# Routed attention and a bilinear feed-forward layer: one product moved to second place at the change of batch element, a combination made later, an assignment spread over two groups, and sums in another order

## The chip, the cores and the metric

The kernel runs on one core of a Trainium2 chip. The metric is the device time of one execution in microseconds (us). The core has TensorE (matrix products, PE in the profile; PEld is its loading of weights), VectorE (DVE), ScalarE (ACT), GpSimd (POOL) and SyncE (SP), which starts most transfers here. SBUF holds the working data, and products land in PSUM.

## The reference

Routed attention: queries and keys get the nearest of 16 centroids of their head, and a query sees only keys of its own centroid. Then a bilinear feed-forward layer.

```python
batch, n_heads, seq, head_dim = (4, 8, 768, 64)   # 16 centroids per head
q_assign = argmax(q_n @ c_n); k_assign = argmax(k_n @ c_n)
scores = where(q_assign == k_assign, q @ k.T / 8, -1e9)
attn = softmax(scores)
x = (attn @ v) laid out as (3072 tokens, 512)
a = x @ w_a            # 512 x 1536
b = x @ w_b
return (a * b) @ w_out # 1536 x 512
```

All of it is float32; the weights come as float64 bits and are rounded on the chip.

## The kernel before

The attention goes over 16 pairs of heads (4 per batch element). A pair has two halves of 384 queries, and a half has six blocks of 128 keys; two blocks make a *group* g, so a pair takes six groups (l = 0 to 5) and the whole attention 96. In group g TensorE makes the scores of g, ScalarE their exponentials, VectorE (from pair 4 on partly GpSimd) adds up the probabilities of g-1, and TensorE weighs the values with them. The feed-forward layer of the batch element before is cut into pieces, which fill TensorE between the groups. The main loop, cut:

```python
for g in range(NG + 3):
    p, l = divmod(g, GPP)                       # GPP = 6 groups per pair
    if l == 0:
        ready = prep_steps(p + 1)               # the next pair's preparation
    ...
    if 0 < g < NG:
        score(now)
    check_inverses()
    if 0 < g <= NG:
        for u in before:
            add_up(u)                           # acc, L570
    flush_w()                                   # end of a weight's rounding
    if 0 < g <= NG:
        weigh(before)
    if g < NG:
        ready[l]()
    late = int(g > EARLY)
    if g % 3 == late and 0 < g - late:
        denominators(*divmod(g // 3 - 1, 2))    # L604
    ...                                         # rounding of weights due now
    if halved:
        todo.extend(normalize(*ph))
    if ffn:
        credit += PER_GROUP[...]
        while len(ffn) > least and credit > 0:
            cost, piece = ffn.popleft()
            credit -= cost
            piece()
            if todo:
                todo.popleft()()
            round_next()
    ...
    while todo:
        todo.popleft()()
    if halved:
        ffn_ready(*ph)                          # a finished element's pieces
```

**Up projection of batch elements 1 to 3.** Blocks of the weights (A) and of x (X) are multiplied by a scheme with seven products instead of eight, for twelve parts (six column blocks of each weight). It needs sums and differences of blocks: S1 to S4 of the weights (a part each) and T1 to T4 of x (once for the batch element). VectorE makes both.

```python
def combine_x(b):                               # the first piece of an element
    up_room()
    x = xTs[b]
    for c in range(2):
        x11, x12 = x[:, c, 0:HB], x[:, c, HB:S]
        x21, x22 = x[:, c + 2, 0:HB], x[:, c + 2, HB:S]
        t2, t3, t4 = (W[t][c] for t in ("T2", "T3", "T4"))
        for out, l, r in ((t3, x22, x12), (x12, x12, x11), (t2, x22, x12),
                          (t4, t2, x21)):
            nc.vector.tensor_tensor(out=out, in0=l, in1=r, op=ALU.subtract)   # L725
```

In the profile T2 and T3 lie in tiles named raw, T4 in size, T1 in xT itself. S1 to S4 are made at L747 (raw, comb, size). The pieces of a part run in the order p1, p6, p2, p7, p4, p5, p3, each with one product (L764) into one of three PSUM buffers (m), which is free again once its result has been added:

```python
def p1():  ps = product("11", "11"); box["11"] = ...; nc.scalar.copy(out=box["11"], in_=ps)
def p6():  ps = product("S2", "T2"); ...; add(box["12"], box["11"], ps)
def p2():  add(box["11"], box["11"], product("12", "21")); done("11", 0, i)
def p7():  ps = product("S3", "T3"); ...; add(box["22"], box["12"], ps)
def p4():  ps = product("22", "T4"); ...; add(box["21"], box["22"], ps, ALU.subtract)
...
for n, (half_1, half_2, ps) in enumerate(parts):
    ps[0] = both(*([half_1] if n == 0 else []), half_2, ps[0])   # S1 to S4 before p1
    if n + 1 < len(parts):
        ps[4] = both(ps[4], parts[n + 1][0])
    pieces += [(2 * HB, f) for f in ps]
```

When a batch element changes, combine_x is put ahead of the last two pieces of the down projection of the element before (L883, additions at L889), and p1 and p6 of the new element follow these:

```python
ffn.insert(len(ffn) - FREE_ROOM, (0, lambda: combine_x(b)))      # FREE_ROOM = 2
ffn.extend(ffn_ups(b, h) + ffn_downs(b, lambda: h))
```

Behind the loop the same pieces run on without attention; between p7 and p4 of the last element's first part one small product (L1109) counts rows that are far off and takes a PSUM buffer of the same three.

**The sums.** For the pairs of the first batch element (p < HP = 4) the last block's probabilities aren't added to acc but summed by TensorE itself, as a second term:

```python
def denominators(p, hf):
    ps = ps_m.tile([P, 512], FP32, name="m")
    acc = accs.pop((p, hf))
    terms = [acc]
    if p < HP:
        terms.append(probs[p * UPP + hf * NJ + NJ - 1])
    for n, t in enumerate(terms):
        for a in range(2):
            nc.tensor.matmul(out=ps[a * D:(a + 1) * D, 0:HB], lhsT=ones,
                             rhs=t[:, a, :], start=(n == 0),
                             stop=(n == len(terms) - 1))              # L604
    den = acc[:, 0, :]
    ...
```

**The assignment.** Pairs from 4 on are prepared by blocks, in six steps, one for each group of the pair before; pair 4's fall into g=18 to 23. Step l=2 has four VectorE instructions (L487, L488, L489, L492), l=3 the one-hot code (half on GpSimd at L470, half on VectorE at L472), l=4 its transpose (L476) and eight transfers to ohT, which the scores of the pair read.

Of the kernel before, what the change touches and what calls it, by code (L numbers as in the profile page):

```python
# [14 lines left out]
ALU = mybir.AluOpType  # L15
AX = mybir.AxisListType
# [120 lines left out]
def short_path(nc, tc, ctx, c, cn, centroids_in, casts, n_far, q, k, v,  # L137
# [3 lines left out]
    B, H, S, D = q.shape  # L141
    NC = 16
    DM, DF = moe_w_a.shape
    NJ = S // P
    HP = H // 2
# [3 lines left out]
    HB = S // 2  # L149
# [93 lines left out]
    first = load_first()  # L243
# [199 lines left out]
    def prep_by_blocks(p):  # L443

        qkTs[p] = qtp.tile([P, 2 * S], FP32, name="qkT")
        ohTs[p] = ohT_bufs[p % 2]
        NG = 24
        QT = slice(0, P // 2)
        KT = slice(P // 2, P)
        shape = (P, NG, NC)  # L450
        sim = simp.tile([P, NG, NC], FP32, name="sim")
        mx = small.tile([P, NG], FP32, name="mx")
        first = small.tile([P, NG], FP32, name="first")
        oh = oh_all[:, 0:3].rearrange("p n (g c) -> p (n g) c", c=NC)
        ohT = oh_all[:, 3:6].rearrange("p n e -> p (n e)")
        top = lambda t: t[:, :, None].broadcast_to(shape)
        v = nc.vector

        def across(w):
            v.transpose(out=qkTs[p][:, w * S:(w + 1) * S],  # L460
                        in_=qks[p][:, w].rearrange("p j d -> p (j d)"))

        def sims_across():
            v.transpose(out=sim.rearrange("p g c -> p (g c)"),
                        in_=sims[p][:, 0:HB])

        def one_hot():


            nc.gpsimd.tensor_tensor(out=oh[KT], in0=sim[KT], in1=top(first)[KT],  # L470
                                    op=ALU.subtract)
            v.tensor_tensor(out=oh[QT], in0=sim[QT], in1=top(first)[QT],  # L472
                            op=ALU.is_equal)

        def one_hot_across():
            v.transpose(out=ohT, in_=oh.rearrange("p g c -> p (g c)"))  # L476
            for a in range(2):
                for kq in range(4):
                    r = 32 * kq + a * NC
                    nc.sync.dma_start(  # L480
                        out=ohTs[p][a * D:a * D + NC, kq * HB:(kq + 1) * HB],
                        in_=ohT[r:r + NC, :])

        return [
            [lambda: across(0), lambda: across(1)],
            [sims_across],
            [lambda: v.tensor_reduce(out=mx, in_=sim, axis=AX.X, op=ALU.max),  # L487
             lambda: v.tensor_tensor(out=sim, in0=sim, in1=top(mx), op=ALU.is_ge),  # L488
             lambda: v.tensor_tensor(  # L489
                 out=sim, in0=sim, in1=rank_far[:, None, :].broadcast_to(shape),  # L490
                 op=ALU.mult),
             lambda: v.tensor_reduce(out=first, in_=sim, axis=AX.X, op=ALU.max)],  # L492
            [one_hot],
            [one_hot_across],
            [],
        ]

    def prep_steps(p):
        if p >= NPAIR:
# [24 lines left out]
    UPP = 2 * NJ  # L524
# [69 lines left out]
    def denominators(p, hf):  # L594


        ps = ps_m.tile([P, 512], FP32, name="m")
        acc = accs.pop((p, hf))
        terms = [acc]
        if p < HP:  # L600
            terms.append(probs[p * UPP + hf * NJ + NJ - 1])
        for n, t in enumerate(terms):
            for a in range(2):
                nc.tensor.matmul(out=ps[a * D:(a + 1) * D, 0:HB], lhsT=ones,  # L604
# [3 lines that stand above are left out]
        n = 4 * p + 2 * hf  # L608
        nc.scalar.activation(out=den, in_=ps[:, 0:HB], func=AF.Copy,
                             accum_out=stat[:, n:n + 1])  # L610
        den_of[p, hf] = acc
# [104 lines left out]
    def combine_x(b):  # L716
        up_room()
        x = xTs[b]
        for c in range(2):
            x11, x12 = x[:, c, 0:HB], x[:, c, HB:S]  # L720
            x21, x22 = x[:, c + 2, 0:HB], x[:, c + 2, HB:S]
            t2, t3, t4 = (W[t][c] for t in ("T2", "T3", "T4"))
            for out, l, r in ((t3, x22, x12), (x12, x12, x11), (t2, x22, x12),
                              (t4, t2, x21)):
                nc.vector.tensor_tensor(out=out, in0=l, in1=r, op=ALU.subtract)  # L725

    def ffn_ups(b, h):
# [3 lines left out]
             "T1": [x[:, c, HB:S] for c in (0, 1)],  # L731
             "21": [x[:, c, 0:HB] for c in (2, 3)],
             "22": [x[:, c, HB:S] for c in (2, 3)]}

        def products(w_sb, i, is_a):
            N2 = NF // 2
            A = {m + n: [w_sb[:, c, f * P:(f + 1) * P] for c in cs]
                 for m, f in (("1", i), ("2", i + N2))
                 for n, cs in (("1", (0, 1)), ("2", (2, 3)))}
            box = {}  # L740

            def combine(name, l, r, op):

                at = {"S1": 1, "S2": 2, "S3": 0, "S4": 3}[name]
                dst = W["slots"][at]
                for c in range(2):
                    nc.vector.tensor_tensor(out=dst[c], in0=l[c], in1=r[c], op=op)  # L747
                A[name] = dst

            def half_1():  # L750
                combine("S1", A["21"], A["22"], ALU.add)
                combine("S2", A["S1"], A["11"], ALU.subtract)

            def half_2():
                combine("S3", A["11"], A["21"], ALU.subtract)
                combine("S4", A["12"], A["S2"], ALU.subtract)
                s = W["slots"]
                W["slots"] = [s[1], s[2], s[0], s[3]]

            def product(l, r):  # L760
                ps = ps_m.tile([P, 512], FP32, name="m")
                rhs = X[r] if r in X else W[r]
                for c in range(2):
                    nc.tensor.matmul(out=ps[:, 0:HB], lhsT=A[l][c], rhs=rhs[c],  # L764
                                     start=(c == 0), stop=(c == 1))
                return ps[:, 0:HB]

            def place(k, f):
                if is_a:
                    return h[k][:, f, :]  # L770
                return hap.tile([P, HB], FP32, name="ha")

            def add(out, in0, ps, op=ALU.add):
                nc.vector.tensor_tensor(out=out, in0=in0, in1=ps, op=op)  # L774

            def done(name, k, f):
                if not is_a:
                    to = h[k][:, f, :]
                    nc.gpsimd.tensor_tensor(out=to, in0=to, in1=box[name],  # L779
                                            op=ALU.mult)  # L780

            def p1():
                if not h:
                    h.extend(hp_.tile([P, NF, HB], FP32, name="h")
                             for _ in range(2))
                ps = product("11", "11")
                box["11"] = place(0, i)
                nc.scalar.copy(out=box["11"], in_=ps)

            def p6():  # L790
                ps = product("S2", "T2")
                box["12"] = place(1, i)
                add(box["12"], box["11"], ps)

            def p2():
                add(box["11"], box["11"], product("12", "21"))
                done("11", 0, i)

            def p7():
                ps = product("S3", "T3")  # L800
                box["22"] = place(1, i + N2)
                add(box["22"], box["12"], ps)

            def p4():
                ps = product("22", "T4")
                box["21"] = place(0, i + N2)
                add(box["21"], box["22"], ps, ALU.subtract)
                done("21", 0, i + N2)

            def p5():  # L810
                ps = product("S1", "T1")
                add(box["12"], box["12"], ps)
                add(box["22"], box["22"], ps)
                done("22", 1, i + N2)

            def p3():
                add(box["12"], box["12"], product("S4", "22"))
                done("12", 1, i)

            return half_1, half_2, [p1, p6, p2, p7, p4, p5, p3]  # L820

        parts = [products(w_sb, i, w_sb is wa_sb) for i in range(NF // 2)
                 for w_sb in (wa_sb, wb_sb)]
        pieces = []
        for n, (half_1, half_2, ps) in enumerate(parts):
            ps[0] = both(*([half_1] if n == 0 else []), half_2, ps[0])
            if n + 1 < len(parts):
                ps[4] = both(ps[4], parts[n + 1][0])
            pieces += [(2 * HB, f) for f in ps]
# [126 lines left out]
    def both(*fs):  # L956
        return lambda: [f() for f in fs]
# [380 lines left out]
```

## Time and profile before

Three runs took 1072.07, 1072.6 and 1073.93 us (median 1072.6). The profiled execution has a span of 1072.3 us and a mean granted TensorE clock of 0.995.

| engine | busy us | share of the span | instructions |
|---|---|---|---|
| VectorE | 708.9 | 66% | 1402 |
| GpSimd | 354.6 | 33% | 329 |
| ScalarE | 260.0 | 24% | 501 |

TensorE's line is shown with the prediction. Transfers take 17.8% of the time of the 16 engines that move data. The first group with feed-forward pieces is g=23, near 117 us; batch elements change near 408, 666 and 904 us.

How to read the lines: `out<-in` names the tiles written and read, the shapes are partitions x elements, `xN` is the number of instructions merged into the line. A float32 product stands as two records, so a product of the up projection with its two chunks has four. The wait in brackets is the idle time ahead of the instruction and what ended it.

### The profile page before, as it was taken

What the parts mean: (1) busy time and instruction counts of PE and PEld (TensorE: products, weight loads), DVE (VectorE), ACT (ScalarE), POOL (GpSimd) and SP (SyncE); (2) the same over time, 40 slices, a digit from 0 to 9 for tenths busy, and PEclk for the clock granted to TensorE, in tenths of its full rate; (3) what the DMA queues carried; (4) which work ended last, traced back from release to release, by engine and by line L of the source; (5) the groups of instructions that cost most, each with busy time, mean ns of one, the idle gap of its engine ahead of it and who ended that gap; (6) DMA issues with size and microseconds to landing.
All of it is one profiled execution on the core that took longest, in us unless ns stands there. A gap on an engine that the chain in (4) does not pass through costs nothing.

```text
span 1072.3 us, 13072 instructions
## 1 busy us (share of the span) xinstructions
PE 1054.1 (98%) x4756; PEld 607.3 (57%) x4756; DVE 708.9 (66%) x1402; ACT 260.0 (24%) x501; POOL 354.6 (33%) x329
## 2 busy tenths in 40 slices
PE   8999999999999999999999999999999999999997
PEld 5444445554557664454545766455455687555686
DVE  5778877787857446666667746667665745676762
ACT  4665333233322221212122121221212200000000
POOL 1111345454533232434445422344344410221200
PEclk9999999999999999999999999999999999999999
DMA  5334243525130210202020030300000000000000
GB/s 169 91 63 108 83 103 101 125 67 139 61 47 20 43 37 14 45 4 45 3 46 1 24 65 14 55 1 19 1 4 1 6 30 25 0 1 1 0 31 32
DMA packets 120504, 46.18 MB, mean 43 GB/s; under 512 B 106608, under 2 KB 115824, under 8 KB 120432
## 3 DMA queue, kind: packets, MB, share of 16 engines
q1 hardware_dynamic: 120016, 44.85, 17.8%
q8 instruction: 39, 0.64, 0.2%
q10 hardware_dynamic: 416, 0.43, 0.1%
q14 instruction: 33, 0.27, 0.1%
HBM read 37.78 MB, written 6.29 MB: 41 GB/s over the span
## 4 chain that ended last, share of the span: by engine, by line
PE 93%; DVE 6%; issue 1%; DMA 0%; POOL 0%; ACT 0%; DVEq 0%; POOLq 0%
PE m L764 30%; PE m L883 19%; PE s L540 14%; PE O L581 12%; PE m L664 12%; PE m L604 3%; PE m L358 1%; DVE raw L725 1%; DVE raw L747 1%; PE m L342 1%; DVE acc L570 0%; DVE xT L725 0%; DVE size L725 0%; DVE ha L774 0%; DVE sim L407 0%
## 5 line engine op out<-in xcount | busy, mean ns | idle before, releaser
L549 ACT ACTIVATE pt<-s 128x768 f32<-128x768 f32 x192 | 145.3, 809 | 314.6 <-PE s L540 260.6
L570 POOL TENSOR_TENSOR acc<-acc,pt 128x384 f32<-128x384 f32 x144 | 152.2, 1071 | 59.7 <-ACT pt L549 43.5
L779 POOL TENSOR_TENSOR h<-h,ha 128x384 f32<-128x384 f32 x72 | 72.7, 1018 | 235.6 <-DVE ha L774 234.1
L581 PE MATMUL O<-pt,v 128*64 128x384 f32 x768 | 145.1, 499 | 0.0
L540 PE MATMUL s<-qkT 64*128 64x384 f32 x768 | 141.1, 487 | 0.0
L774 DVE TENSOR_TENSOR ha<-ha,m 128x384 f32<-128x384 f32 x126 | 66.8, 546 | 74.1 <-PE m L764 73.3
L774 DVE TENSOR_TENSOR h<-h,m 128x384 f32<-128x384 f32 x126 | 67.3, 548 | 71.8 <-PE m L764 71.0
L570 DVE TENSOR_TENSOR acc<-acc,pt 128x384 f32<-128x384 f32 x96 | 73.9, 796 | 37.2 <-POOL acc L570 35.1
L581 PEld LDWEIGHTS O<-pt,v 128*64 128x64 f32 x768 | 46.6, 136 | 86.9 <-issue 85.3
L540 PEld LDWEIGHTS s<-qkT 64*128 64x128 f32 x768 | 71.3, 189 | 32.0 <-issue 1.1
L883 PE MATMUL m<-wo_sb,h 128*128 128x256 f32 x384 | 87.5, 382 | 0.0
L636 POOL TENSOR_TENSOR xT<-xT,acc 128x384 f32<-128x384 f32 x32 | 33.0, 1033 | 153.5 <-DVE acc L631 119.5
L883 PEld LDWEIGHTS m<-wo_sb,h 128*128 128x128 f32 x384 | 72.1, 190 | 16.0 <-issue 4.2
L764 PE MATMUL m<-raw 128*128 128x384 f32 x192 | 70.2, 488 | 0.9 <-DVE ha L774 0.9
L664 PE MATMUL m<-xT,wa_sb 128*128 128x384 f32 x192 | 67.1, 492 | 0.0
L664 PE MATMUL m<-xT,wb_sb 128*128 128x384 f32 x192 | 66.8, 491 | 0.0
L883 PE MATMUL m<-xT,h 128*128 128x256 f32 x288 | 65.4, 382 | 0.1
L883 PEld LDWEIGHTS m<-xT,h 128*128 128x128 f32 x288 | 54.1, 190 | 11.7 <-issue 1.7
L764 PE MATMUL m<-xT,wa_sb 128*128 128x384 f32 x144 | 53.0, 491 | 0.0
L764 PE MATMUL m<-xT,size 128*128 128x384 f32 x144 | 52.8, 490 | 0.0
L764 PE MATMUL m<-xT,wb_sb 128*128 128x384 f32 x144 | 52.8, 490 | 0.0
L664 PEld LDWEIGHTS m<-xT,wa_sb 128*128 128x128 f32 x192 | 35.5, 190 | 29.4 <-issue 3.6
(164 smaller groups left out, 1451.6 us busy)
## 6 DMA issues: line engine op xcount, KB each, us to landing
raw<-in_moe_w_a_dram SPq DMA_DIRECT2D x12, 512.0 KB, 4.3
raw<-in_moe_w_b_dram SPq DMA_DIRECT2D x12, 512.0 KB, 3.5
raw<-in_moe_w_out_dram SPq DMA_DIRECT2D x12, 512.0 KB, 3.2
qk<-in_q_dram SPq DMA_DIRECT2D x48, 96.0 KB, 2.9
qk<-in_k_dram SPq DMA_DIRECT2D x48, 96.0 KB, 3.5
v<-in_v_dram SPq DMA_DIRECT2D x24, 192.0 KB, 3.8
out_dram<-rest SPq DMA_DIRECT2D x24, 128.0 KB, 1.7
v<-in_v_dram SPq DMA_DIRECT2D x4, 384.0 KB, 4.5
```

What stands on the lines that cost most here:

```text
L342: nc.tensor.transpose(out=ps[:, n * P:(n + 1) * P], in_=qks[p][:, w, j].rearrange("p a d -> p (a d)"), identity=ident)
L540: nc.tensor.matmul(out=s[:, a, 0:HB], lhsT=Ts[p][r, S + j * P:S + (j + 1) * P], rhs=Ts[p][r, hf * HB:(hf + 1) * HB], start=start, stop=not ...
L549: nc.scalar.activation(out=pt, in_=s[:, :, 0:HB], func=AF.Exp, scale=SCALE)
L570: eng.tensor_tensor(out=acc[:, a, :], in0=probs[u - 1][:, a, :] if j == 1 else acc[:, a, :], in1=probs[u][:, a, :], op=ALU.add)
L581: nc.tensor.matmul(out=O_of[0][a * D:(a + 1) * D, 0:HB], lhsT=vs[p][:, a, j, :], rhs=probs[u][:, a, :], start=(j == 0), stop=(j == NJ - 1))
L604: nc.tensor.matmul(out=ps[a * D:(a + 1) * D, 0:HB], lhsT=ones, rhs=t[:, a, :], start=(n == 0), stop=(n == len(terms) - 1))
L636: nc.gpsimd.tensor_tensor(out=x, in0=x, in1=den, op=ALU.mult)
L664: nc.tensor.matmul(out=ps[:, 0:HB], lhsT=w_sb[:, ch, f * P:(f + 1) * P], rhs=xTs[b][:, ch, t0:t0 + HB], start=(ch == 0), stop=(ch == NCH - 1))
L764: nc.tensor.matmul(out=ps[:, 0:HB], lhsT=A[l][c], rhs=rhs[c], start=(c == 0), stop=(c == 1))
L774: nc.vector.tensor_tensor(out=out, in0=in0, in1=ps, op=op)
L779: nc.gpsimd.tensor_tensor(out=to, in0=to, in1=box[name], op=ALU.mult)
L883: nc.tensor.matmul(out=ps[:, 0:HN], lhsT=A[l][f // 3][:, f % 3, :], rhs=B[r][f // 2][:, f % 2, :], start=(f == 0), stop=(f == N2 - 1))
```

## The change

It has four parts. (1) In the first part of each batch element's up projection, the product of p2, which reads neither an S nor a T, is made right after p1's, ahead of p6's; its addition stays in p2. (2) T4, which only p4 reads, is made with p2 rather than with the other combinations of x. Both are meant for TensorE's wait when the batch element changes. (3) Pair 4's assignment is spread over two groups, two instructions each, and its one-hot code moves to the group of the transpose. (4) In the sums the last probabilities come first and acc second, so that TensorE can begin before acc is complete.

```diff
-        return [
-            [lambda: across(0), lambda: across(1)],
-            [sims_across],
-            [lambda: v.tensor_reduce(out=mx, in_=sim, axis=AX.X, op=ALU.max),
-             ...                                     # the four, as below
-            [one_hot],
-            [one_hot_across],
-            [],
-        ]
+        assign = [
+            lambda: v.tensor_reduce(out=mx, in_=sim, axis=AX.X, op=ALU.max),
+            lambda: v.tensor_tensor(out=sim, in0=sim, in1=top(mx), op=ALU.is_ge),
+            lambda: v.tensor_tensor(
+                out=sim, in0=sim, in1=rank_far[:, None, :].broadcast_to(shape),
+                op=ALU.mult),
+            lambda: v.tensor_reduce(out=first, in_=sim, axis=AX.X, op=ALU.max)]
+        if p == HP:
+            return [[lambda: across(0), lambda: across(1)], [sims_across],
+                    assign[:2], assign[2:], [one_hot, one_hot_across], []]
+        return [[lambda: across(0), lambda: across(1)], [sims_across],
+                assign, [one_hot], [one_hot_across], []]
...
         if p < HP:
-            terms.append(probs[p * UPP + hf * NJ + NJ - 1])
+            terms.insert(0, probs[p * UPP + hf * NJ + NJ - 1])
...
-            for out, l, r in ((t3, x22, x12), (x12, x12, x11), (t2, x22, x12),
-                              (t4, t2, x21)):
+            for out, l, r in ((t3, x22, x12), (x12, x12, x11), (t2, x22, x12)):
                 nc.vector.tensor_tensor(out=out, in0=l, in1=r, op=ALU.subtract)
...
+        def combine_t4():
+            for c in range(2):
+                nc.vector.tensor_tensor(out=W["T4"][c], in0=W["T2"][c],
+                                        in1=X["21"][c], op=ALU.subtract)
...
+            def p2_ahead():
+                box["P2"] = product("12", "21")
+
             def p2():
-                add(box["11"], box["11"], product("12", "21"))
+                ps = box.pop("P2") if "P2" in box else product("12", "21")
+                add(box["11"], box["11"], ps)
                 done("11", 0, i)
...
-        for n, (half_1, half_2, ps) in enumerate(parts):
+        for n, (half_1, half_2, p2_ahead, ps) in enumerate(parts):
             ps[0] = both(*([half_1] if n == 0 else []), half_2, ps[0])
+            if n == 0:
+                ps[1] = both(p2_ahead, ps[1])
+                ps[2] = both(combine_t4, ps[2])
```

More of the change, by code (lines that the diff above doesn't have):

```diff
@@ L482, in one_hot_across @@
                         in_=ohT[r:r + NC, :])
-        return [
-            [lambda: across(0), lambda: across(1)],
-            [sims_across],
-            [lambda: v.tensor_reduce(out=mx, in_=sim, axis=AX.X, op=ALU.max),
[L488 to L492, printed above, removed]
-            [one_hot],
-            [one_hot_across],
-            [],
-        ]
+        assign = [
[10 more added lines that the diff above has]
+                assign, [one_hot], [one_hot_across], []]
     def prep_steps(p):
@@ L720, in combine_x @@
             x11, x12 = x[:, c, 0:HB], x[:, c, HB:S]
-            x21, x22 = x[:, c + 2, 0:HB], x[:, c + 2, HB:S]
-            t2, t3, t4 = (W[t][c] for t in ("T2", "T3", "T4"))
-            for out, l, r in ((t3, x22, x12), (x12, x12, x11), (t2, x22, x12),
-                              (t4, t2, x21)):
+            x22 = x[:, c + 2, HB:S]
+            t2, t3 = W["T2"][c], W["T3"][c]
+            for out, l, r in ((t3, x22, x12), (x12, x12, x11), (t2, x22, x12)):
                 nc.vector.tensor_tensor(out=out, in0=l, in1=r, op=ALU.subtract)
@@ L818, in p3 @@
                 done("12", 1, i)
-            return half_1, half_2, [p1, p6, p2, p7, p4, p5, p3]
+            return half_1, half_2, p2_ahead, [p1, p6, p2, p7, p4, p5, p3]
         parts = [products(w_sb, i, w_sb is wa_sb) for i in range(NF // 2)
```

## The prediction

> **What bounds the kernel now.** I read the page's busy times first, then TensorE's table of waits, then the timeline around each large wait, and last the granted clock of the stretches behind them. Page part 1 (busy us, share of the span, instructions) and the two largest lines of TensorE's waits (total us, times, longest):
>
> ```profile
> PE 1054.1 (98%) x4756; PEld 607.3 (57%) x4756; DVE 708.9 (66%) x1402; ACT 260.0 (24%) x501; POOL 354.6 (33%) x329
> ```
> ```profile
> PE m L764 <- DVE comb L747: 4.8, 3, 2.2
> PE m L604 <- DVE acc L570: 2.9, 5, 1.7
> ```
>
> TensorE is the bound: of a span of 1072.3 us it is idle for 18.2. No product is added or removed, so only idle time, and time in which it ran slowly, can change. The two lines are what the change aims at: product p6 at the start of a batch element's up projection (L764), and the sums behind the softmax (L604). First the transition to batch element 1 (group g=52), from the timeline (start, us, engine, ..., idle before):
>
> ```profile
> 400.25 3.85 POOL L570 TENSOR_TENSOR acc<-acc,pt 128x384 f32<-128x384 f32 x3
> ...
> 403.28 1.23 DVE L725 TENSOR_TENSOR size<-raw,xT 128x384 f32<-128x384 f32 x1
> ...
> 404.89 1.45 PE L764 MATMUL m<-xT,wa_sb 128*128 128x384 f32 x4
> ...
> 406.20 0.56 DVE L725 TENSOR_TENSOR size<-raw,xT 128x384 f32<-128x384 f32 x1
> ...
> 408.20 0.48 DVE L747 TENSOR_TENSOR comb<-raw,wa_sb 128x128 f32<-128x128 f32 x2
> ...
> 408.54 1.62 PE L764 MATMUL m<-raw,comb 128*128 128x384 f32 x4 [2.20 <-DVE comb L747]
> ...
> 410.09 0.82 PE L540 MATMUL s<-ohT 64*128 64x384 bf16 x4
> ...
> 410.70 2.75 PE L540 MATMUL s<-qkT 64*128 64x384 f32 x8
> ```
>
> TensorE ends p1 at 404.89 + 1.45 = 406.34 and waits 2.20 us for S2 (written to comb), because VectorE still works through the eight subtractions of L725; the two that make T4 (size) are no part of what p6 reads. The last two lines show a second loss: twelve score records that take 1.72 us everywhere else in the chain take 3.30 here. The granted clock (PEclk, the number after the bracket) says why:
>
> ```profile
> core 0: us, PE busy (x), PEclk, DMA share, GB/s
> 408.50:410.00 1.50, 1.46 (x4) 0.97 0.09 23
> 410.00:411.50 1.50, 1.50 (x9) 0.50 0.07 16
> 411.50:413.00 1.50, 1.50 (x8) 0.50 0.09 23
> ```
>
> Then the sums, at g=3 (the same picture stands at g=9 and g=15) and at g=21:
>
> ```profile
> 29.56 1.02 DVE L570 TENSOR_TENSOR acc<-acc,pt 128x384 f32<-128x384 f32 x2
> ...
> 30.16 1.01 PE L604 MATMUL m<-acc,ones 128*64 128x384 f32 x3 [0.32 <-DVE acc L570]
> ```
> ```profile
> 107.98 1.66 DVE L570 TENSOR_TENSOR acc<-acc,pt 128x384 f32<-128x384 f32 x2
> 108.23 0.99 POOL L470 TENSOR_TENSOR oh<-sim,first 64x384 bf16<-64x384 f32 x1 [4.36 <-DVE first L492]
> ...
> 108.58 0.86 PE L604 MATMUL m<-acc,ones 128*64 128x384 f32 x2 [1.67 <-DVE acc L570]
> ...
> 109.70 0.54 PE L604 MATMUL m<-acc,ones 128*64 128x384 f32 x1 [0.26 <-DVE acc L570]
> ```
>
> The sums start with acc, whose last addition VectorE makes after the assignment of the next pair. At g=21 that addition is slow as well: its two halves take 1.66 us, since L470 runs on GpSimd between them.
>
> [...] here a wait of 2.20 us is followed by half clock, and one of 1.67 us (g=21) by clock 1.00. So I take the border to lie between those two. [...] a subtraction takes 1.23 us while L570 runs on GpSimd, 0.56 without. [...] So an early T4 delays S2, and a late T4 delays what stands behind it.
>
> **Part A: product p2 second, T4 later, at g=52 and again 257 us on (batch element 2).** VectorE before: eight subtractions from 399.35, four at about 1.25 us beside GpSimd's additions (which end at 404.10) and four at 0.58 from start to start; then the one-hot transpose and two additions of the down projection; S2 at 408.50. Two subtractions fewer: the first step of the second chunk moves into the slow stretch, so four stay slow, and two quick ones go: 2 x 0.59 = 1.18 us; S2 comes at 407.3. TensorE: p2 needs no combination, only a PSUM buffer, which the down projection's addition frees; that addition moves from 407.17 up to 406.0 and ends near 406.4. So p2 starts at 406.42, where TensorE stood idle, takes 1.29 us (products in a row start 1.29 us apart: 416.22, 417.51, 418.80), and p6 starts at 407.7, after S2. What is left of the wait is 0.1 us, and with it the drop of the clock goes.
> Worth: before, from the end of p1 to the end of the next scores 413.46 - 406.34 = 7.12 us for p6 and scores, whose undisturbed sum is 1.29 + 1.72 = 3.01. Lost: 4.1 (2.20 wait, 0.33 on p6, 1.58 on the scores). Batch element 2, from p1's end at 662.10 + 1.45 to the scores' at 668.57 + 2.11: 7.13, lost 4.1 (2.20, 1.52, 0.39). Gain 4.0 each, **8.0 us**. T4 is made in the next group during the scores (VectorE is free from about 410.2; T4 is done by 411.4 and p2's addition by 412.0), while p4, which reads it and needs p2's buffer, starts near 413.5: hidden.
>
> **Part B: the same at the last transition (901 to 908).** No scores lie between p6 and p7 there. The wait for S2 is only 0.37 us. p2 ahead covers it: p6 at 904.55, p7 at 905.84 to 907.13. But the far-off count's product (L1109) stands behind p7 and takes the PSUM buffer of p2, which is read only after p6's addition (from 905.9, 0.55), two T4 steps (1.15) and its own addition (0.55): free at 908.2. Then p4 starts at 908.35 instead of 907.97: **0.4 us lost**, with a new wait of about 1.0 us, shorter than the 1.67 that left the clock alone.
>
> **Part C: sums as second term, g=3, 9, 15.** From the start of the weighting to the next scores: 32.07 - 28.34 = 3.73 us; where no wait occurs (group at 93.84) it is 2.73. Lost 1.00 each. With the last probabilities first, TensorE has four records (0.65 us) to do from 29.85; acc's first half is there at 30.16, needed at 30.5, the second at 30.63, needed at 30.83. All hidden, and everything around is driven by TensorE itself: **3.0 us**.
>
> **Part D: g=20 to 24.** Before, 111.13 - 105.40 = 5.73, lost 3.0. After: only two of four assignment steps (1.15 us) stand ahead of acc, and L470 is gone from between: acc is complete at 107.95, the sums end at 108.27, the scores of g=22 start 2.9 us earlier. But VectorE is busy without a break from 105 to 113 and its work isn't less. In g=22 the one-hot's GpSimd half now queues behind the weight rounding on GpSimd (1.28 + 1.0 us), and VectorE's transpose waits for it: it starts near 115.1 instead of 113.21. The normalisation (VectorE 1.3 us, GpSimd L636 1.1) behind it ends near 118.3. TensorE would start the first up product at 117.46 - 2.9 = 114.6, do three of its four chunks (1.95 us) and wait for xT from 116.5 to 118.3. Its product then ends at 119.0 against 120.14 before. At g=24 the sums wait some 0.3 us more for acc, VectorE being two us later. I keep **0.8 us** of 2.9.
>
> **Sum.** 8.0 - 0.4 + 3.0 + 0.8 = 11.4; 1072.6 - 11.4 = 1061.2 us.
>
> **Rivals.** *The new wait at g=23 eats more.* For it: 1.8 us lies at the border for the clock (1.67 didn't trip it, 2.20 did); a trip costs about 1.6 us, as above: 1062.8, and 1063.5 if VectorE's lag lasts. Against: my DVE times may be late; with no new wait all 2.9 stay: 1059.1. *S2 remains late at the transitions,* because GpSimd's additions stretch the remaining subtractions further: a residual wait of about 1 us each, clock kept: 1063. Against: these additions end at 404.1 and don't depend on the change. *p2's buffer stalls p4 or p7* in groups 53 and 77 as in part B: p2's addition would have to come 1.5 us later than I work out; at 1 us each 1063.
>
> **Range and chances.** The rivals give 1059 to 1063.5; with a margin for a clock drop more or less, 1058.3 to 1064.5. All idle time of TensorE plus half clock behind the transitions is 18.2 + 3.8 = 22 us; 2% is 21.5, and part of the idle time is the start. So faster by over 2% is close to impossible (0.01), slower by over 2% as well (0.01), since nothing adds 21 us of waits.
>
> **What would show it.** Right: the wait for comb falls from 4.8 to under 0.5 us; scores behind the transitions take 1.72 us at clock 1.00; the waits for acc L570 fall below 1; about 1 us of wait before L1109; a wait of 1 to 2 us for xT (L636) near 116. Wrong: clock 0.50 after either transition, a wait for size or the PSUM buffer in groups 53 or 77, or none near 116.

## The result and the profile after

The changed kernel takes 1064.28 us (median of six runs, 1064.03 to 1065.32) against 1072.02 us of the kernel before in the same six rounds: ratio 0.9929, 95% interval 0.9916 to 0.9942, or 7.7 us faster. Predicted were 11.4 us faster, 1061.2 us, with 1058.3 to 1064.5 as the range. The time lies 0.2 us inside the range's upper end.

TensorE's work is the same 4756 records; the busy times of the changed kernel and those of its waits that bear on the change (page part 1, then the waits: total us, times, longest):

```profile
PE 1049.4 (99%) x4756; PEld 605.4 (57%) x4756; DVE 708.0 (67%) x1402; ACT 260.0 (24%) x501; POOL 354.3 (33%) x329
```
```profile
PE m L767 <- DVE h L777: 0.7, 1, 0.7
PE m L663 <- POOL xT L635: 0.7, 1, 0.7
...
PE m L603 <- DVE acc L569: 0.4, 1, 0.4
PE m L767 <- DVE rest L899: 0.4, 2, 0.2
```

The waits for comb (4.8 us) are gone, and those for acc fell from 2.9 to 0.4. Three small ones are new: ahead of p4 at the last transition (L777), for xT at g=23 (L635), and for p2's buffer at the first two transitions (L899). (Line numbers have moved: L725 is L723 now, L747 L750, L764 L767, L604 L603, L1109 L1119; T4 is made at L735.)

The first transition of the changed kernel, from the timeline (start, us, engine, ..., idle before):

```profile
402.04 1.45 PE L767 MATMUL m<-xT,wa_sb 128*128 128x384 f32 x4
...
403.70 1.56 PE L767 MATMUL m<-xT,wa_sb 128*128 128x384 f32 x4 [0.20 <-DVE rest L899]
...
404.29 0.48 DVE L750 TENSOR_TENSOR comb<-raw,wa_sb 128x128 f32<-128x128 f32 x2
...
405.09 1.45 PE L767 MATMUL m<-raw,comb 128*128 128x384 f32 x4
...
406.81 1.45 PE L539 MATMUL s<-qkT 64*128 64x384 f32 x8
...
407.59 1.02 DVE L735 TENSOR_TENSOR size<-raw,xT 128x384 f32<-128x384 f32 x2
```

p2 stands between p1 and p6, S2 (comb) is complete before p2 ends, the scores run at full clock (PEclk 1.00), and T4 is made beside them, 2.4 us ahead of p4 (408.61 against 411.03). From p1's end (403.49) to the end of the scores (408.27) it takes 4.78 us for p2, p6 and scores, whose undisturbed sum is 4.30.

### The profile page after: what moved, and what is told of

It is laid out like the page before. It is cut to its first block, busy times and chain, and to the rows that moved or that the text cites. A ratio compares the mean times of both kernels' runs of the same rounds, so it can differ in the third digit from the quotient of the medians.

```text
span 1062.4 us, 13065 instructions
## 1 busy us (share of the span) xinstructions
PE 1049.4 (99%) x4756; PEld 605.4 (57%) x4756; DVE 708.0 (67%) x1402; ACT 260.0 (24%) x501; POOL 354.3 (33%) x329
## 4 chain that ended last, share of the span: by engine, by line
PE 93%; DVE 5%; issue 1%; POOL 1%; DMA 0%; ACT 0%; DVEq 0%; POOLq 0%
PE m L767 30%; PE m L893 20%; PE s L539 14%; PE O L580 12%; PE m L663 11%; PE m L603 2%; PE m L358 1%; DVE raw L723 1%; PE m L342 0%; DVE raw L750 0%; DVE acc L569 0%; DVE xT L723 0%; POOL xT L635 0%; DVE ha L777 0%; DMA wo_sb<-in_centroids_dram 0%
## 5 line engine op out<-in xcount | busy, mean ns | idle before, releaser
L777 DVE TENSOR_TENSOR ha<-ha,m 128x384 f32<-128x384 f32 x126 | 66.9, 546 | 74.1 <-PE m L767 73.3
L777 DVE TENSOR_TENSOR h<-h,m 128x384 f32<-128x384 f32 x126 | 67.3, 549 | 64.3 <-PE m L767 63.5
L635 POOL TENSOR_TENSOR xT<-xT,acc 128x384 f32<-128x384 f32 x32 | 32.9, 1029 | 147.9 <-DVE acc L630 121.3
L767 PE MATMUL m<-raw 128*128 128x384 f32 x192 | 70.4, 489 | 0.9 <-DVE ha L777 0.9
L767 PE MATMUL m<-xT,wa_sb 128*128 128x384 f32 x144 | 52.9, 491 | 0.4 <-DVE rest L899 0.4
L767 PE MATMUL m<-xT,size 128*128 128x384 f32 x144 | 52.8, 490 | 0.0
L767 PE MATMUL m<-xT,wb_sb 128*128 128x384 f32 x144 | 52.8, 490 | 0.0
```

What stands on the lines that cost most here:

```text
L635: nc.gpsimd.tensor_tensor(out=x, in0=x, in1=den, op=ALU.mult)
```

## The experiments

Every execution begins with up to 1.5 us that vary: the scores of g=1 start between 18.7 and 20.2 us. In a late start TensorE was slow for longer: the twelve transposes at L342 ahead of 9.9 us take 426 ns each in before_again (20.2) and 282 ns in onehot_early (18.9). The last column takes the start out: it is the profiled span less that start. "Half clock" counts the first two transitions that are followed by PEclk near 0.5 in the profiled execution.

| kernel | median us | before, same chip | ratio, 95% interval | half clock | span - start |
|---|---|---|---|---|---|
| before | 1072.02 | | | 2 | 1072.3 - 19.1 = 1053.2 |
| before_again | 1072.99 | 1073.31 | 0.9996 (0.9988 to 1.0004) | 1 | 1071.7 - 20.2 = 1051.5 |
| changed | 1064.28 | 1072.02 | 0.9929 (0.9916 to 0.9942) | 0 | 1062.4 - 18.7 = 1043.7 |
| a_only | 1066.78 | 1073.31 | 0.9947 (0.9933 to 0.9961) | 0 | 1064.8 - 18.9 = 1045.9 |
| p2_only | 1068.21 | 1073.31 | 0.9953 (0.9940 to 0.9967) | 0 | 1066.4 - 19.1 = 1047.3 |
| t4_only | 1068.85 | 1073.31 | 0.9959 (0.9945 to 0.9972) | 0 | 1067.8 - 20.1 = 1047.7 |
| dummy | 1071.54 | 1072.43 | 0.9994 (0.9986 to 1.0002) | 0 | 1070.3 - 19.8 = 1050.5 |
| c_only | 1068.14 | 1072.43 | 0.9961 (0.9948 to 0.9974) | 0 | 1066.2 - 19.0 = 1047.2 |
| c_shift | 1072.26 | 1072.72 | 0.9996 (0.9987 to 1.0004) | 1 | 1070.3 - 18.9 = 1051.4 |
| no_d | 1064.34 | 1072.43 | 0.9925 (0.9912 to 0.9938) | 0 | 1062.2 - 18.8 = 1043.4 |
| onehot_early | 1063.05 | 1072.43 | 0.9917 (0.9904 to 0.9931) | 0 | 1061.1 - 18.9 = 1042.2 |
| split_first | 1062.39 | 1072.72 | 0.9902 (0.9887 to 0.9917) | 0 | 1061.1 - 20.0 = 1041.1 |
| best | 1061.26 | 1072.72 | 0.9896 (0.9881 to 0.9912) | 0 | 1059.3 - 18.9 = 1040.4 |

**before_again: the kernel before once more.** No edit. The two spans differ by 9.9 us, the medians by 7.7; was the first profiled execution typical?

> The kernel before, once more, to see whether its profiled execution was a typical one: its span was 1072.3 us, but the median over six runs is 1072.0 with 1070.5 to 1073.9, and the median of the changed kernel lies only 7.7 us lower although its span is 9.9 lower. Theory (the half clock follows from the 2.2 us waits in every execution): again both stretches at clock 0.50 behind the two transitions, ratio 1.00. Rival (the half clock comes in some executions only[...]): one or both stretches at full clock, and runs that differ by some 1.9 us steps.

It was not. The wait of 2.2 us stands at both transitions, but only the second is followed by half clock. From the busy times of TensorE by stretches, at the first and the second transition the stretch with the wait and the one behind it (stretch, length, PE busy, PEclk, then the transfers' share and GB/s):

```profile
405.90:409.31 3.41, 1.46 (x5) 1.00 0.00 0
409.31:412.72 3.41, 3.16 (x16) 1.00 0.08 21
661.90:665.31 3.41, 1.21 (x5) 1.00 0.01 4
665.31:668.72 3.41, 3.41 (x10) 0.50 0.07 18
```

At the first, p1's end to the end of the scores is 5.48 us here (407.36 to 412.84) against 7.12: so one stretch of half clock costs 1.64 us. The kernel before has none, one or two of them; without any, its span less the start would be 1053.2 - 2 x 1.64 = 1049.9. The rival was right: of two waits of 2.2 us here only one was followed by half clock. The mean granted clock of each execution says how often: one stretch of 3.41 us at half clock lowers it by 3.41 x 0.5 / 1072 = 0.0016, and of 66 executions of the kernel before in these experiments 9 show 0.999, as without a drop, 47 show 0.997, as with one, and 10 show 0.995 or 0.996, as with two. So one drop is the usual case.

**a_only, p2_only, t4_only: the transitions taken apart.** a_only is parts 1 and 2 of the change without sums and assignment. The other two take one of them each:

```diff
 # p2_only, against a_only: T4 with the other combinations again
-            for out, l, r in ((t3, x22, x12), (x12, x12, x11), (t2, x22, x12)):
+            for out, l, r in ((t3, x22, x12), (x12, x12, x11), (t2, x22, x12),
+                              (W["T4"][c], t2, x[:, c + 2, 0:HB])):
-                ps[2] = both(combine_t4, ps[2])
 # t4_only, against a_only: p2 in third place again
-                ps[1] = both(p2_ahead, ps[1])
```

> Parts 1 and 2 of the change alone (p2 second, T4 later); sums and assignment as before. Theory: 3.6 us at each of the first two transitions (2.0 of the wait, 1.6 of the half clock), 0.15 lost at the last: 7.1 us faster, no wait for comb, scores behind the transitions at clock 1.00. Rival (part of the gain came with VectorE's state left by the other parts): less than 5 us.

> p2 second, but T4 made early as before. Theory (half clock follows only from long waits): S2 comes at the old time; p2 must wait for the down projection's addition to free its buffer, which is as late as before, so TensorE waits about 1.2 us, p6 starts about 0.4 us after S2; gain per transition 0.9 of the wait and 1.6 to 1.9 of the clock, together about 5.3 us, with the last transition 0.3 more. Rival (the clock drops whatever the wait's length): 0.9 per transition, 2.1 us in all.

> T4 later, but p2 third as before. Theory: S2 comes 1.2 us sooner, the wait falls from 2.2 to about 1.0 us and the clock stays at 1.00: 1.2 + 1.8 = 3.0 per transition, 6 us in all, so that p2_only and t4_only together give some 4 us more than both at once (7.1): each alone already saves the clock. Rival (the clock drops whatever the wait's length): 1.2 per transition, 2.4 in all, and the two parts add up.

a_only gained 6.5 us in the median; its profiled execution is 7.3 us below that of before with two half clocks (1053.2 - 1045.9), 4.0 below a kernel before without any (1049.9). p2_only gained 5.1 and t4_only 4.5, together 9.6: 3.0 more than both at once. That overlap was expected (4): either one already shortened the waits so far that no half clock followed. Their waits are as worked out, 1.3 us for p2's buffer and 1.1 us for S2, and the clock behind them is 1.00. From TensorE's waits (total us, times, longest), first p2_only, then t4_only:

```profile
PE m L765 <- DVE rest L896: 2.5, 2, 1.3
```
```profile
PE m L764 <- DVE comb L747: 2.6, 3, 1.1
```

The medians are below what was expected (7.1, 5.3 and 6 us), since not each wait of the kernel before was followed by half clock.

**dummy: the wait shortened by useless work.** At the first two transitions a product that nothing reads stands between p1 and p6.

```diff
+        def idle_product():
+            ps = ps_m.tile([P, 512], FP32, name="m")
+            for c in range(2):
+                nc.tensor.matmul(out=ps[:, 0:HB], lhsT=wa_sb[:, c, 0:P],
+                                 rhs=X["11"][c], start=(c == 0), stop=(c == 1))
...
+            if n == 0 and b < B - 1:
+                ps[1] = both(idle_product, ps[1])
```

> The kernel before with one product more between p1 and p6 at the first two transitions; nothing reads its result, so it only keeps TensorE at work for 1.3 us of the wait. It needs a PSUM buffer that comes free as in p2_only, so TensorE waits 1.2 us, works, and starts p6 some 0.4 us later than before. Theory (a wait of 2.2 us lets the clock drop in part of the executions, one of 1.2 doesn't): no half clock behind the transitions, all runs within about 1 us, near the fastest of before (1070.5 to 1070.9) plus 0.8: 1071.5, so about 1.5 us faster in the median, with more work. Rival (the half clock is no matter of the wait): 0.8 us slower in the median, spread as wide as before (3.6 us).

The median is 0.9 us lower with more work, but the interval includes 1, and the runs spread over 1.8 us (1071.3 to 1073.1; ten of the fourteen are below 1072.1). The times alone don't settle it. The clock does: twelve of the fourteen executions have a mean granted clock of 0.998 or 0.999, as without a drop, against 3 of 19 of the kernel before in the same rounds. The other two (0.997) had a drop somewhere; where, their records don't show. The profiled execution agrees with the theory: waits of 1.3 us, clock 1.00 behind both, and a span less start 0.6 us above the 1049.9 (0.8 expected).

**c_only and c_shift: the sums' order, and the same at the old time.** c_only is part 4 alone. c_shift adds one up product in the first batch element (2.6 us), which nothing reads:

```diff
-            terms.append(probs[p * UPP + hf * NJ + NJ - 1])
+            terms.insert(0, probs[p * UPP + hf * NJ + NJ - 1])
 # c_shift, besides:
         def piece_b(f):
+            if blk == 1 and f == 6:
+                up(wb_sb, f)
             ps = up(wb_sb, f)
```

> The sums' order alone. Theory (acc comes in time for its products but 0.3 us late for the loading of weights ahead of them): 0.66 us at each of g=3, 9, 15 and about 1.0 at g=21, where four records are done within the wait: 3.0 us faster. Rival (all of the 1.0 us hidden, as predicted): 4.0 us.

> The sums' order alone, and one up product more in the first batch element, which nothing reads: 2.6 us of TensorE work, so that the two transitions lie again at the time from the start at which they lay in the kernel before. c_only has both waits of 2.2 us, but no half clock, and its runs all lie at 1067.9 to 1069.0. Theory (whether the clock drops in such a wait hangs on when the wait comes[...]): half clock behind one or both transitions again, median 1072 to 1073, spread over 3 us as before. Rival (chance): no half clock, all runs near 1070.5.

c_only's median is 4.3 us lower, more than either theory said. Its profile gives another size: 1049.9 - 1047.2 = 2.7 us against a kernel before without half clock. The rest is the clock: both waits of 2.2 us are there, unchanged, yet neither is followed by half clock in the profiled execution, and all five runs lie at 1067.9 to 1069.0. All five have a mean clock of 0.998 or 0.999. With 2.6 us of filler the old picture returns: half clock behind the first transition, the median 1072.26, the runs from 1070.6 to 1073.6, a mean clock of 0.997 in nine of the thirteen. From TensorE's waits in c_only, and from the stretches at the first transition in c_shift:

```profile
PE m L764 <- DVE comb L747: 4.8, 3, 2.2
```
```profile
404.86:408.28 3.42, 1.23 (x5) 1.00 0.01 3
408.28:411.69 3.41, 3.41 (x8) 0.50 0.07 19
```

So a shift by 2.6 us, with no change near the wait, changed how often the clock dropped; the rival's picture (no half clock, all runs near 1070.5) did not come. When the drop came can be read from the traces. Each of the four half clocks behind a transition lasted 3.41 us, and in the kernel before the first ends at 413.32 and the second begins at 665.91, 74 lengths of 3.413 us later. So an execution can be divided into windows of this length, laid off from a change of its clock (in c_only from the drop at its end, at 1063.42), and TensorE's idle time in each can be added up. The first transition of the kernel before, and both transitions of c_only:

```profile
406.50:409.91 3.41, 1.37 (x4) 1.00 0.04 11
409.91:413.32 3.41, 3.41 (x13) 0.50 0.07 18
```
```profile
401.23:404.65 3.42, 2.34 (x9) 1.00 0.00 0
404.65:408.06 3.41, 2.30 (x12) 1.00 0.06 14
657.23:660.65 3.42, 1.91 (x7) 1.00 0.00 0
660.65:664.06 3.41, 2.72 (x14) 1.00 0.07 18
```

A wait of 2.2 us that lay within one window left 2.2 us of it idle, and the clock was half in the next (c_shift's first transition, the second of the kernel before and of before_again). Where a border cut the wait, the clock went by the part in each window: at the first transition 3.41 - 1.37 = 2.04 us in one window was followed by the half clock in the kernel before, 1.95 in before_again was not, nor was 1.5 us and less in c_only and at c_shift's second transition. All eight waits follow this. So does the wait of 1.67 us at g=21, in whose window (106.12 to 109.54) TensorE was idle for 1.77 us. From the first full clock on, in none of the thirteen profiled executions was a window with 1.95 us of idle time or less followed by half clock, and each with 2.04 or more was. (The ends of products are modelled in a trace, so the border is rough.) Open is what sets these windows against the kernel: were their phase at the start random, a shift by 2.6 us would not have changed the odds (a mean clock as with a drop in nine of thirteen executions of c_shift, in none of five of c_only). What ties them to it no run here shows.

**no_d and onehot_early: the assignment of pair 4.** no_d is the changed kernel without part 3. onehot_early keeps it, but makes the one-hot code a group earlier:

```diff
-                    assign[:2], assign[2:], [one_hot, one_hot_across], []]
+                    assign[:2], assign[2:] + [one_hot], [one_hot_across], []]
```

> The changed kernel without part 3 (the assignment of pair 4 in one group, its one-hot code a group earlier). Theory (part 3 wins 1.5 us more at g=21 than the sums' order alone would, and gives back 2.1 at g=23 and 24): 0.6 us faster than the changed kernel, near 1063.7; no wait for xT near 116 us and none for acc at g=24, but one of about 1 us for acc at g=21. Rival (part 3 helps, as meant): 0.4 to 0.8 us slower than the changed kernel.

> The changed kernel with the one-hot code in the group of the second half of the assignment instead of with its transpose. Theory (the loss at g=23 and 24 comes from GpSimd's half of the one-hot standing behind the weight rounding there): GpSimd is idle at that time, the transpose starts some 1.7 us earlier, the wait for xT goes (0.95 us won), and that for acc at g=24 shrinks (0.5 to 0.8): 1.5 us faster than the changed kernel, near 1062.8. Rival (VectorE has simply too much to do between g=20 and 24): less than 0.5 us.

no_d has the changed kernel's time (1064.34 against 1064.28): neither the 0.6 us that the theory gave nor the loss of the rival. onehot_early is 1.2 us below it in the median and 1.5 by the last column (1.5 expected). In the profiles, from the scores of g=21 to the first up product of g=24 it takes 129.85 - 103.68 = 26.17 us in the kernel before, 126.96 - 101.44 = 25.52 in no_d, 127.00 - 101.25 = 25.75 in the changed kernel and 125.86 - 101.50 = 24.36 in onehot_early. So the sums' order alone wins 0.65 there, part 3 takes 0.23 of it back, and the one-hot moved earlier turns that into 1.16 more. The reason can be read in the changed kernel's timeline:

```profile
109.71 1.51 POOL L290 TENSOR_TENSOR wb_sb<-wb_sb,rest 128x512 f32<-128x512 f32 x1 [8.27 <-DVE rest L285]
...
111.30 0.84 POOL L470 TENSOR_TENSOR oh<-sim,first 64x384 bf16<-64x384 f32 x1
...
112.17 0.58 DVE L476 STREAM_TRANSPOSE oh<-oh 128x384 bf16<-128x384 bf16 x1 [2.08 <-POOL oh L470]
...
115.44 0.91 PE L663 MATMUL m<-xT,wa_sb 128*128 128x384 f32 x2 [0.68 <-POOL xT L635]
...
125.74 1.33 PE L603 MATMUL m<-acc,ones 128*64 128x384 f32 x4 [0.42 <-DVE acc L569]
```

GpSimd stands idle for 8.27 us, then the rounding (L290) and the one-hot (L470) come at once; VectorE waits 2.08 us for them, and everything behind it is late: the normalisation, for which TensorE waits at 115.44, and acc at 125.74. In onehot_early, in the same view, GpSimd makes the code in its idle time, the transpose starts at 111.05, and the first product has no wait:

```profile
106.87 2.06 POOL L470 TENSOR_TENSOR oh<-sim,first 64x384 bf16<-64x384 f32 x1 [5.17 <-DVE first L490]
...
111.05 0.57 DVE L476 STREAM_TRANSPOSE oh<-oh 128x384 bf16<-128x384 bf16 x1
...
112.82 2.85 PE L663 MATMUL m<-xT,wa_sb 128*128 128x384 f32 x8
```

**split_first and best: what else the findings give.** split_first spreads the assignments of pairs 1 to 3 as well; best also makes the last batch element's T4 early.

```diff
 # split_first, on onehot_early
-            lambda: todo.extend(prep_assign(prep_across(p))),
-            lambda: None,
+            lambda: assigns.extend(prep_assign(prep_across(p))) or
+            todo.extend(assigns[:3]),
+            lambda: todo.extend(assigns[3:]),
 # best, on split_first
-            for out, l, r in ((t3, x22, x12), (x12, x12, x11), (t2, x22, x12)):
+            late = [] if b < B - 1 else [(W["T4"][c], t2, x[:, c + 2, 0:HB])]
+            for out, l, r in [(t3, x22, x12), (x12, x12, x11),
+                              (t2, x22, x12)] + late:
-                ps[2] = both(combine_t4, ps[2])
+                if b < B - 1:
+                    ps[2] = both(combine_t4, ps[2])
```

> The changed kernel with the one-hot code earlier (onehot_early) and the assignments of pairs 1 to 3 also spread over two groups, three instructions and two. Theory: acc is complete 1.1 us sooner at g=3, 9 and 15, before the loading of weights for its products, so the 0.36 us left there go: 1.1 us faster than onehot_early, 1061.9. Rival (what is left there is no wait for acc but the cost of changing operands): no difference.

> split_first, and T4 of the last batch element made with the other combinations, as before, since VectorE has to wait there for the down projection anyway. Theory: the wait of 0.7 us ahead of p4 at the last transition goes, p6 starts no later, since p2 covers S2: 0.6 us faster than split_first, 1061.2. Rival: S2 comes later than p2's end, 0 to 0.3.

By the column without the start, split_first is 1.1 us faster than onehot_early and best another 0.7: both as the theories said (1.1 and 0.6). In the medians it is 0.7 and 1.1; split_first's profiled execution started late (20.0 us), and the starts of the others aren't on record. best, at 1061.26 us (ratio 0.9896, 0.9881 to 0.9912), has the lowest time of all; it was not timed against the changed kernel on the same chip.

## Why the prediction was right, and where its sizes were off

The order of the parts and most of the mechanisms held. What did not is that both drops of the clock come in each execution (A), which PSUM buffer the count of rows takes (B), and when acc is needed (C). Of the missing 3.7 us some 2.0 are sizes of the parts (11.4 against the 9.4 below) and 1.64 is one drop of the clock. That the time still lies within the range is due to the margin for "a clock drop more or less".

*Part A, the first two transitions (predicted 4.0 each).* The wait for S2, its place, T4 hidden behind the scores, and p2's buffer were right. The residue was 0.48 us instead of 0.1: 0.20 waiting for the buffer, the rest in the first records after that gap and at the change to the scores, which I had set at their back-to-back step. That leaves 3.6 each, as the profiles show: 7.12 and 7.13 before, less 3.01 of undisturbed work and less 0.48. But the term that failed most is the half clock in "lost 4.1", some 1.9 us at each transition, counted as if every execution had both drops. I had one profile, and it had both, which 10 of 66 executions have. The reading behind it, that the wait's length decides (a border between 1.67 and 2.20 us), lacked the window: in the profiles the drop went with the idle time within one window of 3.41 us (2.04 us and more, against 1.95 and less). Without drops part A is worth 4.0 us in all (a_only); the clock adds 1.64 for each drop that would have come, mostly one. That is why the profiled spans differ by 9.9 us and the medians by 7.7.

*Part B, the last transition (predicted 0.4 lost).* 0.14 lost: from p1's start to p4's start 6.15 us (891.83 to 897.98) against 6.01 (901.96 to 907.97). The wait came, but ahead of another instruction, as the changed kernel's timeline has it:

```profile
897.08 0.19 PE L1119 MATMUL m<-ones,far_off 128*1 128x1 f32 x2
897.38 1.01 DVE L777 TENSOR_TENSOR h<-h,m 128x384 f32<-128x384 f32 x2
...
897.98 1.56 PE L767 MATMUL m<-size,wa_sb 128*128 128x384 f32 x4 [0.71 <-DVE h L777]
```

The count of rows (L1119) starts before p2's addition (the first of the two at 897.38) has begun, so it does not have p2's buffer; p4 has, and waits for it. "Takes the PSUM buffer of p2" was the step at fault: I had counted the buffers in the order in which they were handed out. With T4 early (best) the wait is gone.

*Part C, sums at g=3, 9, 15 (predicted 1.00 each, "all hidden").* 0.64 each: from the start of the weighting to the next scores 3.09 us (27.89 to 30.98), against 3.73 before and 2.73 undisturbed. I had worked out when the products need acc, but the loading of weights ahead of them (PEld) waited for acc too, 0.34 us at g=3. The changed kernel's timeline at g=3:

```profile
29.23 0.81 PE L603 MATMUL m<-pt,ones 128*64 128x384 f32 x4
...
29.72 0.29 PEld L603 LDWEIGHTS m<-acc,ones 128*64 128x64 f32 x2 [0.34 <-DVE acc L569]
29.88 1.17 PE L603 MATMUL m<-acc,ones 128*64 128x384 f32 x4
```

Four records take 1.17 us instead of 0.81, and no wait of PE is shown: it hides in its busy time. With acc sooner (split_first) the three groups get 1.1 us in all, which is the residue.

*Part D (predicted 2.9 won at g=21, 0.8 kept).* Won 2.5 (5.73 to 3.27 us), kept 0.4: the first up product took 3.63 instead of 2.68 us, and weighting with sums at g=24 3.83 instead of 2.74. The path (GpSimd's rounding ahead of the one-hot, transpose, normalisation, xT) was the predicted one; the wait for xT was 0.7 instead of 1.8, that behind acc 1.1 instead of 0.3. What I had not compared is the right alternative: the sums' order alone wins 0.65 in the same place, so part 3 adds nothing.

The sum, rebuilt for the profiled pair: 2 x 3.6 - 0.1 + 3 x 0.64 + 0.4 = 9.4, and 0.4 for the earlier start: 9.8 of the 9.9 seen. Of the rivals, the new wait at g=23 came, without a drop of the clock; p2's buffer stalled nothing in groups 53 and 77.

## What to carry to other kernels

Before a gain is worked out from one profile, look whether the loss is there in every execution: here a wait of 2.2 us was followed by a half clock worth 1.64 us in half of the cases, and moving the whole kernel by 2.6 us changed how often, since it moved the wait against the windows of 3.41 us. A wait need not vanish to leave the clock alone: shortened to 1.3 us (p2_only), or cut in two by a border (c_only), it did. When work is moved to a later step, look at what queues on each engine in that step; the same code a group earlier, where GpSimd stood idle, was worth 1.4 us that the change had given away. And count when the loading of weights needs its operand, not only the product: at g=3 it waited 0.34 us for acc, and the four records behind it took 1.17 us instead of 0.81.

## What was not expected of the hardware

From the first full clock on, the clock of the thirteen profiled executions was half for one window of 3.41 us after each window in which TensorE had been idle for 2.04 us or more, and after none with 1.95 us or less. Waits of 2.2 us fell on either side, by where the borders of the windows cut them: 4 of 8 were followed by half clock. And at g=3 of the changed kernel a late operand lengthened TensorE's busy time (1.17 us instead of 0.81 for four records) without any wait in its table.
